# Attention and a channel mixer on one core: one more transpose by transfer, five transfers issued on ScalarE's queue, and a re-sorted order of work

## The chip, the cores and the metric

The kernel runs on one core of a Trainium2 chip. The metric is device microseconds of one execution. The names in the profile are PE (TensorE's matmuls), PEld (its weight loads), DVE (VectorE), ACT (ScalarE), POOL (GpSimd) and SP (SyncE, which here only issues transfers). An engine takes its instructions strictly in order, and an instruction that waits for a semaphore holds back all that stand behind it on its engine.

## The reference, cut to what matters

```python
# attention: q, k, v are [4, 8, 768, 64]; every query sees the first 4 keys (the sinks)
# and the last 128 keys up to its own
scores = q @ k.transpose(0, 1, 3, 2) / sqrt(64)
keep = is_sink | in_window
a = softmax(where(keep, scores, -1e9))
x = (a @ v).transpose(0, 2, 1, 3).reshape(4, 768, 512)
# mixer
h = maximum(x.transpose(0, 2, 1) @ w_tok1, 0) @ w_tok2     # over tokens, 768 -> 256 -> 768
u = x + h.transpose(0, 2, 1)
out = u + maximum(u @ w_ch1, 0) @ w_ch2                    # over channels, 512 -> 1536 -> 512
```

## The kernel before

Inputs and outputs are fp32, the matmuls work on bf16. The eight heads of each of the four batches are taken in pairs, so there are 16 pairs; pairs 0 to 3 are batch 0, pairs 4 to 7 batch 1, and so on.

Three ways bring q and k in. Pairs 0 to 3 are loaded as fp32 by transfers on SP's queue (`load_raw`, L125, tile `early`), turned into bf16 by a copy on DVE, ACT or POOL, and transposed on PE. Pairs 4 to 7 are loaded with a cast by transfers on POOL's queue and transposed on PE (L496, four 64x64 corners for each 128x128 block). Pairs 8 to 15 are loaded with a cast and transposed by a transfer on SP's queue (`turned_by_dma`, L450, tiles `qT` and `kT`). Then come the scores on PE into the PSUM tiles `ps_sc` (two of them, each read by one exponential), the exponential on ACT (L612, tile `pT`), and the product with v on PE (tile `x_sb`). The four sink rows of v for batch 0 are fetched by four small transfers into `v_sink_f` (L243); POOL casts them (L173, tile `v_sink`), and later batches copy theirs out of the tile `v_aug`, into which POOL's queue loads v.

The mixer's token step gives `u_sb` in two groups of 256 channels for batches 1 to 3 (four of 128 for batch 0). For the channel step u must stand transposed, as `uT`. Batch 0 and both groups of batch 1 are transposed on PE and copied out of PSUM by ACT or DVE (`turned_u`); both groups of batches 2 and 3 are transposed by a transfer on SP's queue (`transfer_u`, L883). The list `U_BY_DMA` names the (batch, group) that go this way. The first channel product gives `v1T`, 12 blocks by 2 halves of the tokens for each batch; its first matmul for a batch needs both groups of `uT`. The second product is plain for batch 0; for batches 1 to 3 it is done by seven quarter-size products on sums of blocks (`sums_of_v1`, `sums_of_w`). The output leaves by transfers on SP's queue (L1036 for batch 0, L1113 for the others). The last tile of batch 3 leaves in pieces as they are ready: `sc5`, 128 columns of the tile `o_sb`, is the last.

The order on all engines comes from a planner that runs while the program is built. `FIRST_BATCH` lists the PE units of batch 0's attention and token step in order. `MERGED` lists all other PE units: t0 to t73 are attention and token units, c0 to c183 channel units. `LOADS` lists POOL's loads (q, k, v and the weights T, A, C, D). For everything that isn't PE the planner picks engine and place by a cost table with assumed delays; `U_LAG` is what it assumes from the issue of a `uT` transfer to its landing. PE never departs from the listed order. Transfers of SP's and ACT's queues take eight completion semaphores in turn, so a transfer can't be issued before the one eight places earlier has landed.

Of the kernel before, what the change touches and what calls it, by code (L numbers as in the profile page):

```python
# [16 lines left out]
def kernel(  # L17
# [13 lines left out]
    nc = tc.nc  # L31
# [11 lines left out]
    D1 = D + 1  # L43
# [1 line left out]


    MERGED = (
# [11 lines left out]
    )  # L59
    FIRST_BATCH = (  # L60
        "q0 k0 m00 s00 m01 s01 q1 m02 k1 s02 m11 x1 s11 m10 q2 s10 o01 m12 k2 s12 o00 m21 q3 s21 s20 k3 o11 s22 x3 o10 "
# [1 line left out]
        "t21"  # L63
    )
    LOADS = (
        "q4 v1 v2 T0 v3 A0 C3 q5 k4 k5 C1 C0 C2 v4 q6 v5 k6 k7 q7 D2 v6 D1 D0 k8 q8 v7 q9 D3 k9 q10 k11 k10 q11 v8 v9 "
        "q12 k12 v10 v11 k13 q13 k14 q15 v12 q14 v15 v13 k15 v14"
    )
    PRODUCTS = (
        "1a 2a 1b 2b 5a 6a 5b 6b 7a 1c 7b 2c 4a 3a 4b 3b 5c 6c 7c 4c 3c"  # L70
# [6 lines left out]
    NO = 6  # L77
    BY_DMA = 8
    U_LAG = {1: 8000.0, 2: 4000.0, 3: 3500.0}
    U_BY_DMA = [(2, 0), (2, 1), (3, 0), (3, 1)]  # L80

    singles = ctx.enter_context(tc.tile_pool(name="singles", bufs=1))
    qkv_pool = ctx.enter_context(tc.tile_pool(name="qkv", bufs=NQ))
# [18 lines left out]
    in_order = tc.keep_in_program_order  # L102
# [137 lines left out]
    for n in range(4):  # L240
        i, odd = n // 2, n % 2
        rows = slice(D * i + ODD * odd, D * i + ODD * odd + n_sink)
        in_order(nc.sync.dma_start(  # L243
            out=v_sink_f[rows, odd::2, i, 0:D],
            in_=v[0].rearrange("(p o i) s d -> i o s p d", i=2, o=2)[i, odd, 0:n_sink],
        ))
        in_order(nc.vector.memset(v_sink_f[rows, odd::2, i, D:D1], 1.0))
# [564 lines left out]
    def mix_u(b, g, s0, n, by_pe=False):  # L812
        c0, cn = group(b, g)

        def run():
            ps_u = tiles["ps_u", b, g, s0] = bank("mx", n, cn)
            for st in range(n):
                if by_pe:
                    mm(ps_u[:, st], ident, x_sb[b][:, s0 + st, c0:c0 + cn], start=True, stop=False)
                for tt in range(NTOK):  # L820
                    mm(
                        ps_u[:, st], w_tok2[:, tt, ts(s0 + st, P)], tiles["mix", b][0][:, tt, c0:c0 + cn],
                        start=(tt == 0 and not by_pe), stop=(tt == NTOK - 1),
                    )

        def add(e):
            if by_pe:
                return copy(e, u_part(b, g, s0, n), tiles["ps_u", b, g, s0])
            in_order(nc.vector.tensor_tensor(  # L829
                out=u_part(b, g, s0, n), in0=tiles["ps_u", b, g, s0], in1=x_sb[b][:, s0:s0 + n, c0:c0 + cn], op=ALU.add,  # L830
            ))

        op = Op({"DVE": 150.0 + 1.05 * n * cn}, add)
        op.urgent = (1 + g) * (b == 0)
        if by_pe:
            op.cost["ACT"] = 190.0 + 0.78 * n * cn
        done["u", b, g, s0] = op
        return unit(n * (NTOK + by_pe) * cn * 0.422, run, done["h", b, g] + [done["tok2"]], {"mx": [[op]]}, [op])
# [39 lines left out]
    def transfer_u(b, g):  # L878

        for s0, n in [(0, 4), (4, 2)] if g else [(0, NT)]:  # L880
            def run(e, s0=s0, n=n):
                uT = tiles["mix", b][2].rearrange("c (g m p) -> c g m p", g=2, p=P)
                in_order(nc.sync.dma_start(  # L883
                    out=uT[:, g, 2 * s0:2 * (s0 + n)], in_=u_part(b, g, s0, n).rearrange("p t c -> p (t c)"),
                    transpose=True,
                ))

            op = Op({"SP": 230.0 * n + 400.0}, run, [done["u", b, g, u] for u in range(s0, s0 + n, 2)], lag=U_LAG[b])
            op.bulk = 440.0 * n
            for half in range(s0 // QH, (s0 + n - 1) // QH + 1):  # L890
                done.setdefault(("uT", b, half), []).append(op)
            plan.pending.append(op)
# [46 lines left out]
    def attention_and_tokens():  # L939
# [5 lines left out]
        for p in range(first, last + 1):  # L945
# [9 lines left out]
            if p == last:  # L955
                if (b, 0) in U_BY_DMA:
                    transfer_u(b, 0)
# [6 lines left out]
            if hp == 0 and p > first:  # L964
                units.append(mix_h(b - 1, 1, 0, NTOK))
                units += [mix_u(b - 1, 1, st, 2) for st in range(0, NT, 2)]
                if (b - 1, 1) in U_BY_DMA:
                    transfer_u(b - 1, 1)
                else:
                    pieces.append(turned_u(b - 1, 1))  # L970
            if hp == NHP - 1 and p < last:
                if (b, 0) in U_BY_DMA:
                    transfer_u(b, 0)
# [14 lines left out]
        units += [mix_u(b, 1, st, 2) for st in range(0, NT, 2)]  # L988
        if (b, 1) in U_BY_DMA:
            transfer_u(b, 1)  # L990
# [4 lines left out]
    def mix_channels(b):  # L995
        units, parts = [], {}
# [62 lines left out]
        def quartered(b):  # L1059
# [5 lines left out]
            units, made, steps = [], {}, {}  # L1065
# [25 lines left out]
            def columns(n, i):  # L1091
                if b == B - 1 and i == QH - 1 and n in ("3", "8"):
                    return slice(0, QC // 2) if n == "3" else slice(QC // 2, QC)
                return slice(0, QC)
# [13 lines left out]
                    op.deps.append(done[("st", *divmod(before, NT))])  # L1108
                steps[name, i] = op

            def store(st, cols, parts):
                def run(e):
                    in_order(nc.sync.dma_start(  # L1113
                        out=out[b, ds(st * P, P), cols], in_=o_buf[(b * NT + st) % NO][:, cols],
                    ))

                op = Op({"SP": 430.0}, run, parts)
                op.bulk, op.stores = 1.37 * (cols.stop - cols.start), True
                return op

            for i in range(QH):
                lo, hi = i, i + QH
                ends = b == B - 1 and i == QH - 1
                add("r1", i, lo, 0, "X", True)
                add("c1", i, lo, 0, "Z", False)
                add("r2", i, lo, 1, "X", True)
                add("c2", i, lo, 1, "Y", False, columns("3", i))
                if ends:
                    add("c5", i, lo, 1, "Y", False, columns("8", i))
                    steps["c5", i].deps.append(steps["r2", i])  # L1130
                add("r4", i, hi, 1, "X", True)
                add("c4", i, hi, 1, "Y", False)
                add("c3", i, hi, 0, "X", True)
                for later, sooner in (("c1", "r1"), ("c2", "r2"), ("c4", "r4")):
                    steps[later, i].deps.append(steps[sooner, i])
                if ends:
                    for n, st, cols in (
                        ("c1", lo, slice(0, QC)), ("c2", lo, slice(QC, QC + QC // 2)),
                        ("c5", lo, slice(QC + QC // 2, DM)), ("c3", hi, slice(0, QC)), ("c4", hi, slice(QC, DM)),
                    ):  # L1140
                        steps["s" + n, i] = store(st, cols, [steps[n, i]])
                else:
                    for st, parts in ((lo, ("c1", "c2")), (hi, ("c3", "c4"))):
                        steps["s" + parts[0], i] = done["st", b, st] = store(
                            st, slice(0, DM), [steps[n, i] for n in parts],
                        )
# [71 lines left out]
        if b in QUARTERED:  # L1218
            for j in range(0, HF, SUMMED):
                for f0 in (j, j + HF):  # L1220
                    units += [v1(ft, half) for half in range(2) for ft in range(f0, f0 + SUMMED)]
                sums_of_v1(b, j)
            return units + quartered(b)
# [91 lines left out]
    for name in LOADS.split():  # L1315
        kind, n = name[0], int(name[1:])
# [28 lines left out]
    parts = attention_and_tokens()  # L1345
# [47 lines left out]
```

## Time and profile before

| what | value |
|---|---|
| time, median of 3 runs | 195.69 us (195.45 to 195.8) |
| the profiled execution's own time | 194.44 us |
| its span, first to last instruction | 192.7 us |
| granted TensorE clock | 1.000 |
| transfers | 26.34 MB in 82138 packets |
| 128x128 PE matmuls `ps_mx<-uT,w_ch`, 384 columns | 384 of them, 69.2 us busy |

The profile is of one execution. Its page gives the busy share of each engine, then the span in 40 slices of 4.8 us each, in which each digit is the busy share in tenths. A view by windows gives the busy microseconds of each engine in chosen stretches and, in brackets, the number of instructions. The timeline lists instructions with start, length, engine, line and tiles; what stands in square brackets at the end is the idle time of the engine just before and what ended it. The chain of work that ended last runs back from the last instruction through whatever released each step. Matmuls are pipelined, so the length of one matmul in a row is longer than the distance from one to the next.

### The profile page before, as it was taken

To read this page: it belongs to the slowest core of one execution; us is meant where nothing else is said; L and a number is where in the kernel's file an instruction comes from. 1 tells how busy PE (TensorE), PEld (TensorE's weight loads), DVE (VectorE), ACT (ScalarE), POOL (GpSimd) and SP (SyncE) were. 2 spreads that over 40 slices of the span, in tenths; PEclk is the share of its full clock that TensorE was granted. 3 is DMA by queue.
4 is the path that set the end of the run, shared out by engine and by line. 5 is a ranking of instruction groups with operands and counts; after the bars stand their busy time and mean duration, and the time that the engine had idled before them with its cause. 6 is when DMAs were issued, how large, how long until landed. Compare 5 with 4: busy or idle time off the path is not lost.

```text
span 192.7 us, 5797 instructions
## 1 busy us (share of the span) xinstructions
PE 185.8 (96%) x2491; PEld 129.8 (67%) x2491; DVE 134.4 (70%) x299; ACT 106.3 (55%) x183; POOL 60.5 (31%) x78
## 2 busy tenths in 40 slices
PE   6898999999999999999999999999999999999993
PEld 1345995567764564666668888767678886567882
DVE  4768777898976647689778787847678771047672
ACT  4898767878865216879663433778642005764000
POOL 7299663765944951537810000000000000000000
PEclk9999999999999999999999999999999999999999
DMA  5999999999999999999999953400040435000016
GB/s 186 287 293 172 203 202 194 187 194 181 176 122 147 188 186 187 195 184 155 111 138 149 161 117 143 178 0 3 0 82 3 83 112 218 0 0 3 27 67 234
DMA packets 82138, 26.34 MB, mean 137 GB/s; under 512 B 69952, under 2 KB 79296, under 8 KB 82112
## 3 DMA queue, kind: packets, MB, share of 16 engines
q0 software_dynamic: 56864, 11.80, 74.8%
q1 hardware_dynamic: 25248, 14.17, 34.0%
q8 instruction: 19, 0.31, 0.7%
q14 instruction: 7, 0.06, 0.1%
HBM read 26.75 MB, written 6.29 MB: 171 GB/s over the span
## 4 chain that ended last, share of the span: by engine, by line
PE 88%; DMA 6%; DVE 1%; POOL 1%; SPq 0%; ACT 0%; issue 0%
PE ps_mx L164 77%; PE ps_sc L164 9%; DMA early<-in_q_dram 6%; PE ps_sc L496 1%; PE ps_mx L167 1%; PE ps_mx L496 1%; DVE kT L173 0%; SPq L125 0%; POOL k_bf L173 0%; POOL q_bf L173 0%; ACT qT L171 0%; POOL w_tok L182 0%; DVE o_sb L1100 0%; DVE v1T L179 0%; DVE ps_sc L545 0%
## 5 line engine op out<-in xcount | busy, mean ns | idle before, releaser
L164 PE MATMUL ps_mx<-uT,w_ch 128*128 128x384 bf16 x384 | 69.2, 326 | 0.0
L177 ACT ACTIVATE v1T<-ps_mx 128x384 bf16<-128x384 f32 x83 | 40.7, 490 | 36.1 <-PE ps_mx L164 35.5
L612 ACT ACTIVATE pT<-ps_sc 128x1024 bf16<-128x1024 f32 (+1 forms) x48 | 44.2, 954 | 19.6 <-PE ps_sc L164 19.4
L164 PEld LDWEIGHTS <-w_ch 128*128 128x128 bf16 x384 | 35.9, 98 | 21.3 <-issue 0.9
L164 PE MATMUL ps_mx<-w_ch,v1T 128*128 128x256 bf16 (+1 forms) x168 | 29.6, 318 | 0.0
L164 PEld LDWEIGHTS <-v1T 128*128 128x128 bf16 x234 | 22.5, 98 | 10.0 <-issue 0.5
L164 PEld LDWEIGHTS <-early 128*128 128x128 bf16 x222 | 21.3, 98 | 2.8
L164 PEld LDWEIGHTS <-w_tok 128*128 128x128 bf16 x240 | 19.5, 98 | 3.6 <-issue 0.2
L157 POOL DMA_DIRECT2D v_aug<-in_v_dram x16 | 16.7, 1050 | 7.5 <-PE ps_mx L164 5.1
L1255 DVE TENSOR_TENSOR early<-v1T 128x1152 bf16<-128x1152 bf16 x12 | 8.9, 754 | 13.8 <-ACT v1T L177 13.6
L829 DVE TENSOR_TENSOR u_sb<-ps_mx,x_sb 128x512 bf16<-128x512 f32 (+1 forms) x24 | 15.4, 654 | 2.9 <-PE ps_mx L164 2.6
L148 POOL DMA_DIRECT2D q_bf<-in_q_dram x16 | 13.2, 827 | 12.2 <-DMA q_bf<-in_q_dram 4.0
L164 PE MATMUL ps_mx<-w_sums,early 128*128 128x256 bf16 x126 | 15.9, 273 | 0.0
L164 PE MATMUL ps_mx<-v_aug,pT 128*128 128x65 bf16 x352 | 15.6, 193 | 0.0
L1100 DVE TENSOR_TENSOR o_sb<-ps_mx,u_sb 128x256 f32<-128x256 f32 x28 | 11.7, 422 | 5.3 <-PE ps_mx L164 5.1
L148 POOL DMA_DIRECT2D k_bf<-in_k_dram x16 | 13.3, 840 | 6.6 <-DMA v_aug<-in_v_dram 3.3
L164 PEld LDWEIGHTS <-pT 128*128 128x128 bf16 x352 | 13.8, 97 | 2.3 <-issue 0.4
L620 DVE TENSOR_TENSOR pT<-pT,mask_main 128x768 bf16<-128x768 bf16 (+1 forms) x25 | 14.6, 614 | 0.3 <-ACT pT L612 0.3
L164 PE MATMUL ps_sc<-qT,kT 64*32 64x160 bf16 (+3 forms) x480 | 14.2, 233 | 0.4 <-DVE ps_sc L545 0.2
L164 PE MATMUL ps_mx<-h1T,w_tok 128*128 128x256 bf16 (+1 forms) x120 | 14.2, 251 | 0.0
L164 PEld LDWEIGHTS <-kT 64*32 64x32 bf16 (+1 forms) x512 | 7.0, 91 | 9.1 <-issue 8.0
L164 PE MATMUL ps_mx<-x_sb,w_tok 128*128 128x256 bf16 (+1 forms) x120 | 12.2, 251 | 0.0
(84 smaller groups left out, 201.8 us busy)
## 6 DMA issues: line engine op xcount, KB each, us to landing
out_dram<-o_sb SPq DMA_DIRECT2D x22, 256.0 KB, 2.8
v_aug<-in_v_dram POOLq DMA_DIRECT2D x16, 192.0 KB, 9.4
w_ch<-in_moe_w_ch_dram POOLq DMA_DIRECT2D x8, 384.0 KB, 10.4
early<-in_q_dram SPq DMA_DIRECT2D x4, 384.0 KB, 5.2
early<-in_k_dram SPq DMA_DIRECT2D x4, 384.0 KB, 6.4
k_bf<-in_k_dram POOLq DMA_DIRECT2D x16, 96.0 KB, 11.3
q_bf<-in_q_dram POOLq DMA_DIRECT2D x16, 96.0 KB, 8.8
q_bf<-in_q_dram POOLq DMA_DIRECT2D x4, 192.0 KB, 9.4
```

What stands on the lines that cost most here:

```text
L148: in_order(nc.gpsimd.dma_start(out=out[:, h], in_=rows[:, h]))
L157: in_order(nc.gpsimd.dma_start(out=v_aug.rearrange("p i t d -> p (i t) d")[:, :, 0:D], in_=v[b].rearrange("h s d -> (h s) d")[2 * hp * S:2 ...
L164: in_order(nc.tensor.matmul(*args, skip_group_check=True, **kwargs))
L167: in_order(nc.tensor.transpose(out, in_, ident))
L177: in_order(nc.scalar.activation(out, in_, AF.Relu))
L496: in_order(nc.tensor.transpose(outs[x][columns], block, ident[rows, rows]))
L612: in_order(nc.scalar.activation(part(tiles["pT", p][:, :, ds(2 * g, 2)]), of_keys(tiles["ps_s", p, g])[:, :, 0:width(g)], AF.Exp, scale=scale,
L620: in_order(nc.vector.tensor_tensor(out=pt, in0=pt, in1=m, op=ALU.mult))
L829: in_order(nc.vector.tensor_tensor(out=u_part(b, g, s0, n), in0=tiles["ps_u", b, g, s0], in1=x_sb[b][:, s0:s0 + n, c0:c0 + cn], op=ALU.add,))
L1100: in_order(nc.vector.tensor_tensor(out=o_sb, in0=ps, in1=u_rows(b, st)[:, g, cols] if first else o_sb, op=ALU.add,))
L1255: lambda e, n=n, x=x, y=y, how=how: in_order(nc.vector.tensor_tensor(out=v1_sums[:, n, ds(j, SUMMED)], in0=of(x), in1=of(y), op=how,)), deps,
```

## The change

There are four edits.

1. `U_BY_DMA` gains (1, 0): group 0 of batch 1's u is transposed by one transfer of 12 blocks on SP's queue. The 48 matmuls of 64x64 columns on PE and the two copies out of PSUM go.
2. The four loads of the sink rows are issued by ACT instead of SP.
3. The last store, `sc5`, is issued by ACT instead of SP.
4. `MERGED` and `LOADS` are new lists of the same units and loads. `FIRST_BATCH` and `PRODUCTS` are as before.

```diff
     MERGED = (
-        "t0 t1 c20 t2 c23 c11 c22 t3 c16 c6 c0 t7 c17 c9 c1 c10 t4 c14 t5 c2 c4 t6 c5 t8 c12 t10 c21 c8 t9 t11 c13 c7 "
+        "t1 t0 c8 t2 c9 c4 c17 t3 c0 c6 c23 t7 c19 c20 c7 c2 t4 c18 c14 t5 c12 c5 t6 t8 c3 t10 c15 t9 c21 c22 t11 c1 "
...
     LOADS = (
-        "q4 v1 v2 T0 v3 A0 C3 q5 k4 k5 C1 C0 C2 v4 q6 v5 k6 k7 q7 D2 v6 D1 D0 k8 q8 v7 q9 D3 k9 q10 k11 k10 q11 v8 v9 "
+        "k4 v1 v2 T0 v3 A0 q4 C1 k5 C0 q5 C2 C3 v4 v5 q6 k7 k6 v6 q7 D0 q8 D3 k8 D1 v7 D2 q9 k9 q10 k10 q11 k11 v8 v9 "
...
-    U_BY_DMA = [(2, 0), (2, 1), (3, 0), (3, 1)]
+    U_BY_DMA = [(1, 0), (2, 0), (2, 1), (3, 0), (3, 1)]
...
-        in_order(nc.sync.dma_start(
+        in_order(nc.scalar.dma_start(
             out=v_sink_f[rows, odd::2, i, 0:D],
...
-            def store(st, cols, parts):
+            def store(st, cols, parts, by="SP"):
                 def run(e):
-                    in_order(nc.sync.dma_start(
+                    in_order((nc.scalar if by == "ACT" else nc.sync).dma_start(
                         out=out[b, ds(st * P, P), cols], in_=o_buf[(b * NT + st) % NO][:, cols],
                     ))
 
-                op = Op({"SP": 430.0}, run, parts)
+                op = Op({by: 430.0}, run, parts)
...
-                        steps["s" + n, i] = store(st, cols, [steps[n, i]])
+                        steps["s" + n, i] = store(st, cols, [steps[n, i]], "ACT" if n == "c5" else "SP")
```

The start of ACT's program before, with the semaphores waited for (DMAHW is a transfer's landing, PE and DVE are those engines):

```order
L171 ACT_TABLE_LOAD
L171 ACTIVATE q_bf<-early 128x2x6x64 [waits DMAHW0_49]
L171 ACTIVATE qT_129<-ps_mx 128x384 [waits PE_49] x2
L171 ACTIVATE kT_125<-ps_mx 128x384 [waits PE_49] x2
L612 ACTIVATE pT_133<-ps_sc_73 128x2x512 [waits PE_49]
```

The same place in the changed program:

```order
L243 DMA v_sink_f<-in_v_dram 4x2x64 [waits DVE_49]
L243 DMA v_sink_f<-in_v_dram 4x2x64 x3
L171 ACT_TABLE_LOAD
L171 ACTIVATE q_bf<-early 128x2x6x64 [waits DMAHW0_49]
L171 ACTIVATE qT_129<-ps_mx 128x384 [waits PE_49] x2
L171 ACTIVATE kT_125<-ps_mx 128x384 [waits PE_49] x2
L612 ACTIVATE pT_133<-ps_sc_73 128x2x512 [waits PE_49]
```

The four loads stand ahead of the load of ACT's function table, and the first of them waits for DVE's memset of `v_sink_f`; the table load and the first cast, `q_bf`, stand behind them.

SP's program around the new transfer of batch 1 (`qT_131` and `kT_127` are pair 10's, `qT_132` and `kT_128` pair 11's):

```order
 L450 DMA_TRANSPOSE kT_126<-k_bf 128x6x128
+L1036 DMA out_dram<-o_sb_104 128x512
+L450 DMA_TRANSPOSE qT_131<-q_bf 128x6x128
+L883 DMA_TRANSPOSE uT<-u_sb 128x12x128
+L450 DMA_TRANSPOSE kT_127<-k_bf 128x6x128
+L1036 DMA out_dram<-o_sb_102 128x512
 L1036 DMA out_dram<-o_sb_103 128x512
-L450 DMA_TRANSPOSE qT_131<-q_bf 128x6x128
+L450 DMA_TRANSPOSE qT_132<-q_bf 128x6x128
 L450 DMA_TRANSPOSE kT_128<-k_bf 128x6x128
```

The new transfer stands right behind pair 10's `qT` and ahead of pair 10's `kT`, in a row of transfers that wait for loads and for stores' data.

The end of SP's program (the pieces of the last output tiles):

```order
 L1113 DMA out_dram<-o_sb_105 128x512
-L1113 DMA out_dram<-o_sb_101 128x512
 L1113 DMA out_dram<-o_sb_103 128x128
 L1113 DMA out_dram<-o_sb_102 128x512
 L1113 DMA out_dram<-o_sb_106 128x256
-L1113 DMA out_dram<-o_sb_103 128x128
 L1388 UNCONDITIONAL_BRANCH
```

The last 128x128 store leaves SP's queue; on ACT it stands behind the last `v1T`, with nothing after it.

More of the change, by code (lines that the diff above doesn't have):

```diff
@@ L65 @@
     LOADS = (
-        "q4 v1 v2 T0 v3 A0 C3 q5 k4 k5 C1 C0 C2 v4 q6 v5 k6 k7 q7 D2 v6 D1 D0 k8 q8 v7 q9 D3 k9 q10 k11 k10 q11 v8 v9 "
-        "q12 k12 v10 v11 k13 q13 k14 q15 v12 q14 v15 v13 k15 v14"
+        "k4 v1 v2 T0 v3 A0 q4 C1 k5 C0 q5 C2 C3 v4 v5 q6 k7 k6 v6 q7 D0 q8 D3 k8 D1 v7 D2 q9 k9 q10 k10 q11 k11 v8 v9 "
+        "q12 k12 v10 v11 q13 k13 v12 v15 k15 v13 k14 q14 q15 v14"
     )
```

20 rows, old and new, of the table MERGED are left out of this document.

## The prediction

> **What bounds the kernel now.** I read the page first: the busy shares, the slices and the chain that ended last.
>
> ```profile
> span 192.7 us, 5797 instructions
> PE 185.8 (96%) x2491; PEld 129.8 (67%) x2491; DVE 134.4 (70%) x299; ACT 106.3 (55%) x183; POOL 60.5 (31%) x78
> PE   6898999999999999999999999999999999999993
> PE 88%; DMA 6%; DVE 1%; POOL 1%; SPq 0%; ACT 0%; issue 0%
> ```
>
> PE is the bound: 96% busy, nine tenths or more in nearly every slice after the fourth, and 88% of the chain. The other engines matter only where PE waits for them. A busy PE could still hide waits, so I read the view by windows, first in steps of 2 us over the start, then in long stretches. Columns: window, its length, then busy us and instruction count of PE, PEld, DVE, ACT and POOL, the clock, the DMA share and GB/s.
>
> ```profile
> 8.00:10.00 2.00, 1.69 (x27) 0.66 (x24) 1.79 (x4) 2.00 (x5) 0.90 (x2) 1.00 1.73 260
> 10.00:12.00 2.00, 2.00 (x36) 0.92 (x33) 0.54 (x2) 2.00 (x4) 2.00 (x3) 1.00 1.34 265
> 12.00:14.00 2.00, 2.00 (x42) 1.07 (x39) 1.95 (x6) 2.00 (x4) 1.85 (x3) 1.00 1.34 334
> 14.00:16.00 2.00, 1.14 (x45) 0.76 (x44) 1.16 (x3) 1.12 (x3) 2.00 (x3) 1.00 2.40 165
> 16.00:18.00 2.00, 1.78 (x42) 1.30 (x43) 1.91 (x5) 2.00 (x4) 2.00 (x4) 1.00 1.62 191
> 18.00:20.00 2.00, 2.00 (x39) 1.34 (x36) 1.97 (x6) 1.83 (x3) 2.00 (x4) 1.00 1.98 178
> 57.00:78.00 21.00, 21.00 (x323) 11.54 (x304) 13.57 (x28) 8.08 (x11) 11.43 (x13) 1.00 1.89 174
> 78.00:108.00 30.00, 30.00 (x380) 21.27 (x378) 23.80 (x48) 20.39 (x37) 11.44 (x13) 1.00 2.04 153
> 108.00:189.00 81.00, 81.00 (x855) 62.06 (x853) 52.93 (x115) 34.57 (x64) 0.00 (x0) 1.00 0.26 73
> ```
>
> Two things follow. From about 18 us to the end PE has no gap to give back: a microsecond that PE loses or saves there is a microsecond of the span. And from 8 to 14 us ACT is busy without a break; in the next 2 us it is not. So the start has a second engine at its limit, and the change puts work on exactly that engine.
>
> **The sink rows on ACT's queue.** The timeline of the start, and of 18 to 20 us:
>
> ```profile
> 0.74 1.28 ACT L171 ACT_TABLE_LOAD   x1 [0.74 <-PEq L1374]
> 2.26 0.47 SPq L125 DMA_DIRECT2D early<-in_k_dram  x1
> 2.29 0.49 DVE L239 MEMSET v_sink_f<- 128x520 f32 x1
> 2.81 1.36 SPq L243 DMA_DIRECT2D v_sink_f<-in_v_dram  x4
> 3.85 0.84 ACT L171 ACTIVATE q_bf<-early 128x768 bf16<-128x768 f32 x1 [1.83 <-DMA early<-in_q_dram]
> 4.22 0.40 SPq L125 DMA_DIRECT2D early<-in_q_dram  x1
> 9.10 0.61 POOL L173 CAST v_sink<-v_sink_f 128x520 bf16<-128x520 f32 x1 [3.51 <-DMA v_sink_f<-in_v_dram]
> 13.39 0.84 ACT L612 ACTIVATE pT<-ps_sc 128x768 bf16<-128x768 f32 x1
> 13.86 0.82 POOL L173 CAST q_bf<-early 128x768 bf16<-128x768 f32 x1
> 15.12 0.49 ACT L171 ACTIVATE qT<-ps_mx 128x384 bf16<-128x384 bf16 x1 [0.88 <-PE ps_mx L505]
> 15.51 1.94 ACT L612 ACTIVATE pT<-ps_sc 128x1024 bf16<-128x1024 f32 x2
> 17.68 0.84 ACT L612 ACTIVATE pT<-ps_sc 128x768 bf16<-128x768 f32 x1
> 18.69 0.61 PE L164 MATMUL ps_sc<-qT,kT 64*128 64x256 bf16 x8
> 19.18 1.94 ACT L612 ACTIVATE pT<-ps_sc 128x1024 bf16<-128x1024 f32 x2 [0.17 <-PE ps_sc L164]
> ```
>
> Before, ACT loads its function table at 0.74, is done at 2.02 and idles 1.83 us until the first q has landed; the table load costs nothing. In the changed order the four loads stand ahead of it and the first waits for DVE's memset, which ends at 2.78. SP issues the four from 2.81 to 4.17, 1.36 us. At that price ACT's table load runs from 4.17 to 5.45, and the first cast starts at 5.45 instead of 3.85: **ACT begins 1.60 us late**. Queued behind it are all of ACT's work of the first batch, and PE and DVE, which wait for each of its results in turn.
>
> What takes this back is ACT's own idle time. There is none until 14.23 (13.39 + 0.84), then 0.88 before 15.12 and 0.17 before 19.18: 1.05 us together. The 0.88 is a wait for PE, which waited for POOL's cast of the last q (13.86) and so for a load that does not move. So the exponential at 17.68 starts 1.60 - 0.88 = 0.72 late, and the scores that PE writes at 18.69 into the PSUM tile that this exponential reads (free at 17.68 + 0.84 = 18.52, 0.17 ahead) start 0.72 - 0.17 = **0.55 us late**. From there on PE has no gap, so this stays.
>
> Bounds: the trace has no transfer issued by ACT. If ACT issues at no more than 0.2 us each, the delay stays inside 1.05 and nothing is lost: 0. If each issue costs what SP takes for a big load, 0.47, the four take 1.9 and the loss is 1.1. I take 0.55, because the same four transfers are the nearest row. On the other side of the ledger SP is relieved of 1.36 us, but its next load (4.22) waits anyway for the first q to land, which released ACT at 3.85; at most 0.37 is won on one load, and the loads share one stream. Worth nothing in the sum. POOL's cast of the sink rows had waited 3.51 for them and may come earlier; POOL's next hard wait, the load behind 13.86, stays.
>
> **The transpose by transfer.** The chain shows the turned group as one piece, and the groups by line the copies that go with it:
>
> ```profile
> 57.23 0.53 PE ps_mx L496 x48
> L171 ACT ACTIVATE uT<-ps_mx 128x768 bf16<-128x768 bf16 x3 | 2.3, 823 | 0.0
> ```
>
> PE loses 48 matmuls and 48 weight loads, **-0.53 us** in a stretch where PE is the bound. The two copies, some 0.8 us each on ACT, lay beside PE's work (ACT is busy 8.08 of 21 us there) and bring nothing. The price is the transfer's landing. Rows of SP's queue, of the first `uT` product of batch 1 on PE, and of the median time from issue to landing:
>
> ```profile
> 53.97 1.29 DVE L829 TENSOR_TENSOR u_sb<-ps_mx,x_sb 128x512 bf16<-128x512 f32 x2 [1.05 <-PE ps_mx L164]
> 62.77 1.82 SPq L450 DMA_TRANSPOSE qT<-q_bf  x1
> 64.75 1.30 SPq L450 DMA_TRANSPOSE kT<-k_bf  x1
> 77.56 1.64 PE L164 MATMUL ps_mx<-uT,w_ch 128*128 128x384 bf16 x9
> qT<-q_bf SPq DMA_TRANSPOSE x8, 7.8
> uT<-u_sb SPq DMA_TRANSPOSE x6, 3.7
> ```
>
> u is complete at 55.3 before. The new order puts its last third behind a handful of output units, a few us later, still ahead of 62.77, where pair 10's `qT` gets its data. The `uT` transfer stands behind that one, so it is issued at about 64.65. It must have landed by 77.56: 12.9 us. Six-block transposes of that busy time land 7.8 us after issue; the quiet `uT` ones, late in the kernel, 3.7. This one has twelve blocks in the busy time, so between 7.8 and 15.6; the middle, 11.7, is in time by 1.2 us. I take 0. At the far end PE stands 15.6 - 12.9 = 2.7 us.
>
> **The last store.**
>
> ```profile
> 189.40 0.28 DVE L1100 TENSOR_TENSOR o_sb<-ps_mx,o_sb 128x128 f32<-128x128 f32 x1
> 189.51 0.33 SPq L1113 DMA_DIRECT2D out_dram<-o_sb  x1
> 189.94 0.40 SPq L1113 DMA_DIRECT2D out_dram<-o_sb  x1
> ```
>
> Its data are there at 189.68, but SP is still at the store before (189.51 + 0.33) and issues it at 189.94. An idle ACT can issue at about 189.73: **-0.2 us**; bounds are 0, where the two stores then land together, and -0.26.
>
> **The re-sorted lists.** They hold the same units with the same work, so PE's sum doesn't change; PE waits for nothing in 57 to 189 us now, so they can only add waits. I take 0. A possible place is an ACT wait such as this one, which PE did not feel:
>
> ```profile
> 106.87 0.53 ACT L171 ACTIVATE v_sink<-v_aug 4x65 bf16<-4x65 bf16 x2 [2.13 <-DMA v_aug<-in_v_dram]
> ```
>
> **The sum.** +0.55 - 0.53 - 0.2 = -0.18 us on the profiled execution, 194.44 to 194.26. The median of the runs is 195.69, 1.25 above that execution; the difference carries over, 195.5. A measurement of this kernel can tell about 0.2%, 0.39 us, from no change.
>
> **The rivals.**
>
> *Late table (slower).* The gap between 2.02 and 3.85 on ACT could hide more of the table load than its row of 1.28 shows. Once the load stands directly ahead of the first cast, whatever was hidden, up to 1.83 us, comes on top and goes straight to PE, since the 1.05 is used up: -0.18 + 1.83 = +1.65 at the far end, and with half of it, 0.92, +0.7. It decides as soon as more than 0.6 us was hidden. For it speaks only that the trace cannot exclude it; against it that no instruction stands in the gap. [...] The middle case's time is 195.69 + 0.7 = 196.4.
>
> *Late uT (slower).* The transfer shares its queue with stores and pair 10's and 11's transposes, and lands after PE gets to its first product. For it: 1.2 us of room against an uncertainty of several. Against: the listed order was made with a delay in view. Half of the 2.7: -0.18 + 1.35 = +1.2, 196.9. It decides when the transfer takes longer than 12.9 us.
>
> *Cheap issue (faster).* ACT's issues cost little, the delay at the start stays within 1.05 us, and only the gains remain: -0.53 - 0.2 = -0.73, 195.0. It decides at 0.2 us for each issue (2.81 + 0.8 + 1.28 = 4.89, which is 1.04 late). For it: only SP's price is known, and ACT may be quicker. Against: the same hardware path is asked for.
>
> *Another wait of the new order (slower).* A load or transpose that comes later by the new transfer's time holds ACT or PE: by half of the 2.13 that ACT already waits, about +0.9 in all, 196.6.
>
> **How the numbers follow.** Balance, my forecast: 0.35; its own range, with the issue from 0.3 to 0.47 us, is 195.3 to 196.1. Late table 0.15, late `uT` 0.17, other wait 0.13, cheap issue 0.2. Faster by over 0.2% is cheap issue and a twentieth from the balance: 0.25. Within 0.2% is nearly all the rest of the balance, 0.3. Slower is the remainder, 0.45: three separate mechanisms, none of which is likely alone. The range must reach the cheap issue at 195.0 with 0.1 below it, and the middles of the three slower cases, up to 196.9, with a little beyond: 194.9 to 197.1; the far ends of late `uT` and late table, about one in ten, are left out.
>
> **What would show it.** In the changed profile: the table load on ACT should start near 4.2 us and the first `q_bf` cast near 5.5 with no idle time between; PE's gap-free run should begin about half a microsecond later, with a wait for ACT at 17 to 19 us; 48 matmuls fewer on L496; no idle PE at the first `ps_mx<-uT,w_ch` of batch 1 near 77.6, with `uT` landing before it; the last store issued by ACT some 0.05 us after DVE's last addition. Idle time between the table load and the cast would speak for the late table; a cast before 5 us for the cheap issue; an idle PE anywhere after 20 us proves the zero that I took for transfer and order wrong.

## The result and the profile after

The changed kernel takes 197.95 us in the median (196.34 to 200.74, 11 executions) against 195.54 for the kernel before (11 executions beside it): a ratio of 1.0103, 95% interval 1.0079 to 1.0127. (Ratios compare undisturbed executions alone, so they are not quite the ratio of the medians.) That is slower by over 0.2%, 2.45 us above the forecast of 195.5 and above the top of its range, 197.1. The profiled execution took 197.05 us, 2.6 above the one before (194.44). The page:

```profile
span 195.3 us, 5700 instructions
PE 186.7 (96%) x2443; PEld 129.6 (66%) x2443; DVE 134.3 (69%) x301; ACT 104.1 (53%) x179; POOL 60.6 (31%) x78
PE   6698999999999999999999999999999999999993
PE 88%; DVE 5%; ACT 4%; issue 1%; ACTq 1%; DVEq 0%
```

PE is still the bound, but ACT now stands on the chain with 4% where it had 0%, and the second slice of PE reads 6 where it read 8. So the loss begins in the first 10 us. The chain of waits has one long piece that both kernels share, 77 matmuls without a wait, first before and then after:

```profile
21.57 3.85 PE ps_mx L164 x77
```
```profile
23.95 3.85 PE ps_mx L164 x77
```

By there PE is **2.38 us late**. The rest of the span adds little: 0.53 comes back where the 48 transposes are gone, 0.25 is lost near 45 us and 0.5 in the last 10 us (2.38 - 0.53 + 0.25 + 0.5 = 2.60, and the spans differ by 195.3 - 192.7 = 2.6). The start, by the timeline:

```profile
2.81 1.53 ACTq L243 DMA_DIRECT2D v_sink_f<-in_v_dram  x4
4.38 1.28 ACT L171 ACT_TABLE_LOAD   x1 [4.38 <-issue]
5.67 0.84 ACT L171 ACTIVATE q_bf<-early 128x768 bf16<-128x768 f32 x1
6.57 0.50 PE L505 MATMUL ps_mx<-ident,q_bf 64*128 64x64 bf16 x12 [1.94 <-ACT q_bf L171]
7.32 1.03 PE L164 MATMUL ps_sc<-mask_add,ident 128*128 128x512 bf16 x2
8.29 0.97 POOL L173 CAST v_sink<-v_sink_f 128x520 bf16<-128x520 f32 x1 [2.90 <-DMA v_sink_f<-in_v_dram]
9.06 1.02 ACT L612 ACTIVATE pT<-ps_sc 128x1024 bf16<-128x1024 f32 x1 [0.32 <-PE ps_sc L164]
18.20 0.22 PE L164 MATMUL ps_mx<-v_sink,pT_sink 128*128 128x130 bf16 x1 [0.45 <-DVE kT L173]
19.84 0.40 PE L164 MATMUL ps_mx<-qT,kT 64*32 64x512 bf16 x4 [0.67 <-DVE pT L620]
```

ACT does what the prediction said: issues, table load, cast, one behind the other, the cast at 5.67 where it was at 3.85. New are two things. PE stands still for 1.94 us (its "hole") between its warm-up, dummy matmuls that keep it busy before there is data, and its first transpose. And it is *slow* there: the two `mask_add` matmuls take 1.03 us. Before, the first transposes and the same two matmuls were:

```profile
4.78 0.51 PE L505 MATMUL ps_mx<-ident,q_bf 64*128 64x64 bf16 x12
5.82 0.61 PE L164 MATMUL ps_sc<-mask_add,ident 128*128 128x512 bf16 x2
```

The hole did not make PE slow in this execution. Its first transposes take 0.50 us, as before (0.51), and in executions in which PE was at full rate there they take 0.35 (s5 below). PE works slowly from the start: its warm-up weight loads begin 0.43 us apart in the changed kernel, and in s5 so up to 3.99, where from 4.38 on four take 0.75 us. So PE had not yet reached its full rate in either; before it got there by 5.82 (0.61), here only near 10 us (the transposes at 10.22 take 0.34). ACT, which was to catch up in its idle time, now waits for a slow PE (0.32 at 9.06, another 0.34 at 10.43). And PE waits for DVE at 18.20 and 19.84, where before it waited for nothing.

The transfer, by the instructions on the tile `uT`, and the first channel product of batch 1 by the timeline:

```profile
L883 SPq DMA_TRANSPOSE uT<-u_sb x1: 4982/4982/4982, 65.3 to 65.3; - x1
DMA to landing us min/median/max: 11.1/11.1/11.1
```
```profile
79.73 2.45 PE L164 MATMUL ps_mx<-uT,w_ch 128*128 128x384 bf16 x14
```

It lands at 65.3 + 11.1 = 76.4, some 3.3 us before PE asks for it, and PE does not wait. Near 45 us, the chain:

```profile
42.94 0.97 DVE kT L173
44.04 0.38 DVE ps_sc L545
44.42 0.46 DVE v1T L179
```

DVE has a long copy and a memset of PSUM to do one behind the other, where before the memset began at 41.67, well ahead; the copy out of PSUM that PE waits for (`v1T`) comes behind both. The end, by the timeline:

```profile
188.39 0.42 DVE L1100 TENSOR_TENSOR o_sb<-ps_sc,o_sb 128x256 f32<-128x256 f32 x1 [0.89 <-PE ps_sc L164]
189.50 0.50 PE L164 MATMUL ps_mx<-w_ch,early 128*128 128x128 bf16 x6
190.18 0.81 PE L164 MATMUL ps_sc<-w_ch,early 128*128 128x256 bf16 x6 [0.18 <-DVE o_sb L1100]
192.03 0.28 DVE L1100 TENSOR_TENSOR o_sb<-ps_mx,o_sb 128x128 f32<-128x128 f32 x1
192.35 0.39 ACTq L1113 DMA_DIRECT2D out_dram<-o_sb  x1
```

Here DVE first has nothing to do for 0.89 us, then too much at once, and PE waits for it. The last store leaves ACT 0.04 us after the last addition, yet the span ends 195.3 - 192.31 = 3.0 us behind that addition, as it did before (192.7 - 189.68).

### The profile page after: what moved, and what is told of

The parts are those of the page before. It is cut to its first block, busy times and chain, and to the rows that moved or that the text cites. A ratio compares the mean times of both kernels' runs of the same rounds, so it can differ in the third digit from the quotient of the medians.

```text
span 195.3 us, 5700 instructions
## 1 busy us (share of the span) xinstructions
PE 186.7 (96%) x2443; PEld 129.6 (66%) x2443; DVE 134.3 (69%) x301; ACT 104.1 (53%) x179; POOL 60.6 (31%) x78
## 4 chain that ended last, share of the span: by engine, by line
PE 88%; DVE 5%; ACT 4%; issue 1%; ACTq 1%; DVEq 0%
PE ps_mx L164 75%; PE ps_sc L164 11%; DVE kT L173 2%; ACT qT L171 1%; ACT pT L612 1%; PE ps_sc L496 1%; PE ps_mx L167 1%; PE ps_mx L505 1%; ACT L171 1%; PE ps_mx L496 1%; DVE o_sb L1100 1%; ACTq L243 1%; DVE v1T L179 0%; ACT q_bf L171 0%; ACT kT L171 0%
## 5 line engine op out<-in xcount | busy, mean ns | idle before, releaser
L164 PE MATMUL ps_mx<-uT,w_ch 128*128 128x384 bf16 x384 | 68.0, 326 | 0.1
L157 POOL DMA_DIRECT2D v_aug<-in_v_dram x16 | 16.6, 1042 | 11.8 <-DVE v1T L179 5.3
L1100 DVE TENSOR_TENSOR o_sb<-ps_mx,u_sb 128x256 f32<-128x256 f32 x28 | 11.8, 421 | 6.8 <-PE ps_mx L164 6.7
L164 PE MATMUL ps_mx<-v_aug,pT 128*128 128x65 bf16 x352 | 16.1, 193 | 0.0
```

Source lines behind the costliest of these rows:

```text
L157: in_order(nc.gpsimd.dma_start(out=v_aug.rearrange("p i t d -> p (i t) d")[:, :, 0:D], in_=v[b].rearrange("h s d -> (h s) d")[2 * hp * S:2 ...
L164: in_order(nc.tensor.matmul(*args, skip_group_check=True, **kwargs))
L1100: in_order(nc.vector.tensor_tensor(out=o_sb, in0=ps, in1=u_rows(b, st)[:, g, cols] if first else o_sb, op=ALU.add,))
```

## The experiments

Each kernel was run beside the kernel before, whose median was 195.7 to 196.1 in these comparisons; ratios are to it, with 95% intervals.

**One part at a time.** Four kernels take the change apart: the sink loads alone (before, with `nc.scalar` for `nc.sync` in the loop that loads `v_sink_f`), the changed kernel without them, the transfer alone, and the last store alone.

```diff
 s1_only_sinks    (before)   -        in_order(nc.sync.dma_start(     # v_sink_f
                             +        in_order(nc.scalar.dma_start(
 s2_sinks_back    (changed)  -        in_order(nc.scalar.dma_start(   # v_sink_f
                             +        in_order(nc.sync.dma_start(
 s3_only_ut       (before)   -    U_BY_DMA = [(2, 0), (2, 1), (3, 0), (3, 1)]
                             +    U_BY_DMA = [(1, 0), (2, 0), (2, 1), (3, 0), (3, 1)]
 s4_only_store    (before)   +    ... store(st, cols, [steps[n, i]], "ACT" if n == "c5" else "SP")
```

> The kernel before with one edit: the four sink-row loads issued by ACT. Every other engine's order is the same as before. Theory S (the start): ACT's table load falls behind the issues, the first cast starts at 5.6 to 5.7 us instead of 3.85, and the gap-free run of PE begins 2.4 us later; nothing gives it back, so +2.4 us, about 1.2% slower. Theory L (the new lists carry the loss, and part of the late start comes from the units they put there): a loss of 0.55 us as forecast, at most 1.1, so 0.3 to 0.6% slower.

> The changed kernel with the sink-row loads back on SP, all else as changed. Theory S: the start is as before; what is left is -0.5 for the transposes, +0.2 to 0.3 for a wait near 44 us and +0.5 for waits among the last products, so +0.2 us against before, the same within 0.2%. Theory L: 1.3 to 1.9 us slower than before still.

> The kernel before with one edit: group 0 of batch 1 turned by the transfer, lists as before. If the saved PE work counts in full and the transfer lands before the first product of batch 1: -0.5 us, 0.25% faster. The rival of a late transfer: PE stands at the first product of batch 1 near 77 us by up to 2.7 us, a net of 0 to +2.2 us.

> The kernel before with one edit: the last 128-column store issued by ACT. By the forecast's term -0.2 us (0.1%). By the changed kernel's trace, where ACT issued 0.04 us after the last addition but the end lay 3.0 us behind that addition as before: 0.

| kernel | median us | ratio |
|---|---|---|
| s1, sink loads alone | 197.55 | 1.0117 (1.0082 to 1.0153) |
| s2, all but the sink loads | 195.98 | 1.0025 (0.9992 to 1.0059) |
| s3, transfer alone | 196.29 | 1.0037 (1.0010 to 1.0064) |
| s4, last store alone | 195.85 | 1.0012 (0.9983 to 1.0042) |

The loss is the sink loads. Moving one small group of transfers costs 1.2%; everything else together costs too little to tell from nothing. The last store shows no gain, though its interval leaves room for the 0.2 us of the forecast. The transfer alone is slower by 0.4%, where a gain of 0.25% was forecast. In its trace the time of the 48 matmuls is won (0.51), and PE does not wait for `uT`, and yet DVE and PE wait later for loads on POOL's queue:

```profile
80.86 0.38 DVE L173 COPY v_sink<-v_aug 4x65 bf16<-4x65 bf16 x2 [2.43 <-DMA v_aug<-in_v_dram]
86.03 0.30 PE L164 MATMUL ps_mx<-v_sink,pT_sink 64*128 64x65 bf16 x8 [1.42 <-DVE x_sb L722]
```

Whether the transfer's traffic made these loads late is not shown: this execution, at 197.78, was the slowest of twelve.

**Why the start costs three times the forecast.** Two theories. *Late ACT*: everything queues behind ACT's late cast. *Clock*: PE loses its granted clock in the hole of about 2 us. The trace of s1, by windows (the column behind POOL is the clock):

```profile
6.00:8.00 2.00, 1.06 (x26) 0.52 (x26) 0.58 (x3) 1.56 (x4) 0.00 (x0) 0.93 1.07 335
8.00:10.00 2.00, 1.72 (x10) 0.42 (x12) 1.12 (x2) 1.63 (x3) 0.67 (x2) 0.50 1.68 239
10.00:12.00 2.00, 2.00 (x34) 1.06 (x30) 0.62 (x2) 1.44 (x3) 2.00 (x3) 0.50 1.34 280
12.00:14.00 2.00, 1.64 (x13) 0.37 (x10) 2.00 (x3) 1.38 (x3) 1.79 (x2) 0.50 1.43 319
14.00:16.00 2.00, 2.00 (x38) 1.04 (x35) 0.73 (x2) 2.00 (x4) 1.57 (x3) 0.87 2.30 172
```

Here, other than in the changed kernel's trace, PE had the full clock (0.60 for the two `mask_add` matmuls at 7.04), lost it just behind the hole, and had half of it until after 14 us. The next two kernels are s1 with one part of the mechanism taken away: s5 fills the hole with more warm-up matmuls and leaves ACT late; s6 lets ACT load its table first and so starts the cast at 4.40.

```diff
 s5_sinks_warm (s1)   -    keep_warm(7, 0)
                      +    keep_warm(12, 0)
 s6_sinks_table (s1)  +    table = singles.tile([P, 1], BF16)
                      +    in_order(nc.scalar.activation(table, ones[:, 0:1], AF.Copy))
```

> Before with the four sink loads on ACT, and 12 warm-up matmuls instead of 7, so that PE does not stand still while the cast is late. Theory late ACT: the loss of the sink edit (2.3 us in the run with that edit alone) is ACT's late cast and what queues behind it; PE's idle time meant nothing, and the time stays near 198.0, perhaps 0.2 more for the longer warm-up. Theory clock: about half of the loss, 1.0 to 1.3 us, is PE at half speed from 7.7 to 14.5 us because it had stood still for 2 us; with the hole filled PE is at full speed by about 9 us, and the time is 196.6 to 197.0.

> Before with the four sink loads on ACT, and one ACT copy of a single column of ones ahead of them, so that the function table is loaded before the loads are issued. Both theories of the start agree that the first cast then comes at about 4.35 instead of 5.67 (0.5 late against before), which is inside ACT's idle 1.05 us. Late ACT: at most 0.3 us over before, 195.7 to 196.1. Clock: PE still stands still 0.5 us longer than before, which can cost the full clock in more of the executions: 196.0 to 196.6. If it stays at 198 the issues cost something else than the place of the table load.

s5 takes 195.87 us, ratio 1.0006 (0.9978 to 1.0035): no loss is left to see, though ACT's cast is as late as in s1 (5.69). s6 takes 196.31, ratio 1.0010 (0.9971 to 1.0049). In s5 PE is at full speed at once behind a hole of half the length (lines between these are left out):

```profile
6.58 0.35 PE L505 MATMUL ps_mx<-ident,q_bf 64*128 64x64 bf16 x12 [0.96 <-ACT q_bf L171]
7.04 0.60 PE L164 MATMUL ps_sc<-mask_add,ident 128*128 128x512 bf16 x2
19.53 0.61 PE L164 MATMUL ps_sc<-qT,kT 64*128 64x256 bf16 x8
```

Neither theory gave a number as low as 195.87 for s5; the clock theory had the sign right and half of the size.

**The hole without a late ACT.** s10 is the kernel before with a shorter warm-up; nothing but PE is touched.

```diff
 s10_cold (before)    -    keep_warm(7, 0)
                      +    keep_warm(3, 0)
```

> Before with 3 warm-up matmuls instead of 7 and nothing else: no engine but PE is touched, ACT's first cast stays at 3.85, and PE stands still for about 1.9 us ahead of its first real matmul. Theory clock: the hole alone costs what the sink edit cost; PE is at half speed until 10 us or later, and the time is 196.8 to 197.8. Theory late ACT: with ACT in time nothing is lost, 195.5 to 196.0.

195.81 us, ratio 0.9996 (0.9967 to 1.0025). The clock theory said 196.8 to 197.8 and **is wrong as it stood**: a hole of 1.93 us costs nothing while ACT is in time.

**Both together, without any transfer on ACT's queue.** If neither a late ACT nor a hole costs anything alone, either the two cost it together, or the transfers on ACT's queue do something of their own. s14 makes ACT late by six needless copies; s15 is the same with the hole filled; s16 is the whole change with the table loaded first, as in s6.

```diff
 s14_act_busy (before)        +    for _ in range(6):
                              +        in_order(nc.scalar.activation(o_buf[NO - 1], ones, AF.Copy))
 s15_act_busy_warm (s14)      -    keep_warm(7, 0)
                              +    keep_warm(12, 0)
```

> Before with six needless ACT copies of ones (into an output tile that is overwritten later) ahead of the first cast; the sink loads stay on SP. ACT is then free for the first cast at about 5.7 to 5.9 instead of 3.85, as late as with the sink loads on its queue. Theory both (a late ACT and PE's hole of 2 us together cost the clock): 197.3 to 198.2. Theory queue (the transfers on ACT's queue do something more than delay): 195.9 to 196.6, the price of the late ACT alone.

> The same with 12 warm-up matmuls, so that PE has next to no hole. Theory both: the loss goes, 195.8 to 196.3. Theory queue: no difference between this kernel and the one without the longer warm-up.

> The changed kernel with one ACT copy of a single column ahead of its four sink loads, so that the function table is loaded first; the first cast comes at 4.4 instead of 5.67, PE's hole is 0.7 instead of 1.94 us. Theory both: as with the sink edit alone, where this took 1.2 us away, 196.3 to 196.8, and what is left over before is half ACT's 0.5 and the new order's waits of 0.7 less the transposes' 0.5. If the table's place is not the cause: 197.8 to 198.1.

With before, s10 and s13 (below) this is a table of two causes, each there or not. The last column counts executions whose mean granted clock was under 0.995.

| kernel | ACT's first cast | PE's hole | median us | ratio | low clock |
|---|---|---|---|---|---|
| s13 | in time (3.92) | 0.15 | 195.68 | 0.9991 (0.9968 to 1.0014) | 1 of 12 |
| s10 | in time (3.96) | 1.93 | 195.81 | 0.9996 (0.9967 to 1.0025) | 0 of 12 |
| s15 | late (5.89) | 0.66 | 196.00 | 1.0016 (0.9986 to 1.0046) | 0 of 12 |
| s14 | late (5.89) | 2.14 | 197.64 | 1.0102 (1.0068 to 1.0136) | 6 of 10 |

So it is the two together, whatever makes ACT late. s14 has no transfer on ACT's queue and costs what the change costs. But the number of warm-up matmuls sets two things, the hole and how long PE has been busy ahead of it. No run with an ACT as late changes one without the other, so "hole" in this table stands for both.

The low clock goes with the loss: 6 of 11 executions of the changed kernel, 4 of 6 of s1, 7 of 12 of s7 (below), and none of 36 of the three kernels with ACT as late and the hole filled (s5, s11, s15). The kernel before has it in 10 of the 125 executions beside these. Where it lies is known for the profiled executions alone: behind the hole in s1 and s14, in the changed kernel's nowhere in its first 190 us, and in s7's only from 20.8 to 24.2 us, where PE had waited for DVE for 0.45 and 1.05 us:

```profile
20.00:22.00 2.00, 1.57 (x16) 0.86 (x17) 1.26 (x4) 0.84 (x2) 1.22 (x2) 0.69 1.30 201
22.00:24.00 2.00, 1.72 (x21) 1.18 (x22) 0.32 (x1) 1.01 (x2) 0.82 (x2) 0.50 1.30 202
24.00:26.00 2.00, 2.00 (x37) 1.66 (x35) 1.44 (x5) 1.28 (x3) 1.02 (x1) 0.96 1.32 203
```

Two places in the timeline show how the two add up: the first small product on the sinks, and the scores that before were written at 18.69. Before (the first place), s10 (hole), s15 (late ACT) and s14 (both), in this order, with the lines between left out:

```profile
9.81 0.40 PE L164 MATMUL ps_mx<-qT,kT 64*32 64x512 bf16 x4
```
```profile
6.27 1.04 PE L164 MATMUL ps_sc<-mask_add,ident 128*128 128x512 bf16 x2
11.43 0.41 PE L164 MATMUL ps_mx<-qT,kT 64*32 64x512 bf16 x4
19.46 0.61 PE L164 MATMUL ps_sc<-qT,kT 64*128 64x256 bf16 x8
```
```profile
11.41 0.40 PE L164 MATMUL ps_mx<-qT,kT 64*32 64x512 bf16 x4
19.71 0.61 PE L164 MATMUL ps_sc<-qT,kT 64*128 64x256 bf16 x8
```
```profile
7.22 0.61 PE L164 MATMUL ps_sc<-mask_add,ident 128*128 128x512 bf16 x2
9.00 1.03 PE L164 MATMUL ps_sc<-mask_add,ident 128*128 128x512 bf16 x2
12.62 0.41 PE L164 MATMUL ps_mx<-qT,kT 64*32 64x512 bf16 x4
20.92 0.61 PE L164 MATMUL ps_sc<-qT,kT 64*128 64x256 bf16 x8
```

Against the execution before, s10 is 1.62 late and then 0.77; s15 1.60 and then 1.02; s14 2.81 and then 2.23. Each delay alone finds 0.6 to 0.85 us of idle time to hide in. Together they find 0.58 in all: the slack is there once. But s10's delay is not its hole's own: s4, in which nothing at the start was touched, shows the same `mask_add` row and is 1.55 and then 1.22 late (11.36 and 19.91). What s10 stands for here is a PE that reaches its full rate late.

s2 and the changed kernel, which differ in the sink loads alone, say the same. In both profiled executions PE is slow at first (1.03 for the `mask_add` matmuls); the first cast comes at 4.00 and 5.67, and the 77 matmuls begin at 22.20 and 23.95. Of ACT's 1.67 us nothing is absorbed. In s11, the changed kernel with 12 warm-up matmuls and PE at full rate (below), they begin at 22.96. So what decides is whether PE is at full rate while ACT should catch up. With 7 warm-up matmuls and a late ACT it had not reached it (the changed kernel, s7) or lost it again (s1, s14); with 12 it had it in all three traces (s5, s11, s15).

s16 takes 196.68, ratio 1.0036 (1.0004 to 1.0068): 1.3 us of the change's loss go with the place of the table load alone.

**The changed kernel with the hole filled, and the lists of before.**

```diff
 s11_after_warm (changed)  -    keep_warm(7, 0)
                           +    keep_warm(12, 0)
 s7_lists_back (changed)   MERGED and LOADS of before
```

> The changed kernel with 12 warm-up matmuls instead of 7. Theory clock: what it lost over before goes as it went with the sink edit alone (197.55 to 195.87, so -1.7); the transposes' -0.5 and the new order's waits of 0.7 stay: 196.0 to 196.4, and 0.3 above the kernel with the sink edit and 12 warm-ups at most. Theory late ACT: 197.6 to 198.2, as the changed kernel.

> The changed kernel with the lists MERGED and LOADS of before. Theory lists help the transfer: without the new order the uT transfer pushes back POOL's loads of v, as it did in before with the transfer alone; the time is that of the sink edit plus the transfer, 197.6 + 0.6 = 198.2 to 198.8, above the changed kernel's 197.95. Theory lists hurt: the new order only added waits (0.25 at 45 us, 0.5 at the tail); then this is 197.2 to 197.5, below the changed kernel.

s11: 196.34 us, ratio 1.0034 (1.0009 to 1.0059), so five more warm-up matmuls take 1.6 us from the median of the changed kernel (0.7%, some 1.35 us, by the ratios). s7: 197.66, ratio 1.0076 (1.0043 to 1.0108), between what the two theories gave, and its interval overlaps the changed kernel's: whether the new lists help or hurt is **not settled**. The waits for v that s3's trace shows are not in s7's profiled execution, so they do not come every time with the transfer and these lists.

**A better version.** s9 puts the last 22 channel units of s2 back into the order that before has; s12 adds two warm-up matmuls to it, and s13 adds the same two to before.

```diff
 s9_tail (s2)              c162 to c183 of MERGED in before's order
 s12_best (s9)             -    keep_warm(7, 0)
                           +    keep_warm(9, 0)
 s13_before_warm (before)  the same
```

> The changed kernel with the sink loads back on SP, and the last 22 channel units (c162 to c183) in the order that before has. Theory tail: the 0.5 us that PE and DVE lose from 185 us on comes from c173 standing late among these units; it goes, and the time is 195.98 - 0.45 = 195.5 (195.3 to 195.7), with no PE wait for DVE's o_sb in the last 8 us. Theory elsewhere: the tail's loss belongs to something earlier (a late transfer or copy), and the time stays at 195.9 to 196.1.

> The sink loads back on SP, the last 22 channel units in before's order, the transfer for u and the last store as changed, and 9 warm-up matmuls instead of 7. Theory clock: two more matmuls fill the 0.2 to 0.5 us holes ahead of the first transposes, the full clock comes by 8 us in more executions, and up to 1.2 us goes against 0.3 us of later start: 194.8 to 195.3, with fewer executions above 196. If the clock's moment does not depend on holes this small: 195.9 to 196.1.

> Before with 9 warm-up matmuls instead of 7 and nothing else. Theory clock: 195.0 to 195.5 with fewer executions above 196, 0.2 to 0.3 above the kernel with the same warm-up that also saves the 48 transposes. If holes this small do not matter: 195.9 to 196.2, by the later start.

s9: 195.75, ratio 0.9984 (0.9955 to 1.0014); the time lies between the two forecasts and does not decide. In its tail the two products that stood 0.68 us apart in the changed kernel (189.50 and 190.18) follow each other in 0.33 with no wait:

```profile
188.56 0.50 PE L154 MATMUL ps_mx<-w_ch,early 128*128 128x128 bf16 x6
188.89 0.82 PE L154 MATMUL ps_sc<-w_ch,early 128*128 128x256 bf16 x6
```

s12: 195.38, ratio 0.9981 (0.9957 to 1.0006); s13: 195.68, ratio 0.9991 (0.9968 to 1.0014). Both medians lie between what the two theories gave. s12 beats the changed kernel clearly (1.0103 against 0.9981); that it beats the kernel before is likely but not shown.

## Why the prediction was wrong

**The start, +0.55: this is the step that failed.** Its parts were right one by one. The four issues took 1.53 us on ACT (1.36 taken from SP), the cast came 1.82 late (1.60), and with PE at full clock its subtraction comes out in s5 and s15, which have before's lists. In s5 ACT is 1.84 late (5.69) and the scores of 18.69 come 0.84 late (19.53), where 1.84 - 1.05 = 0.79; in s15 it is 2.04 (5.89) and 1.02, where 2.04 - 1.05 = 0.99. What failed is that the 1.05 us of idle time can be taken off at all in most executions. Two things were not in it. PE's hole was not looked at: the prediction followed ACT's lateness along ACT and asked of PE only when it would get its data, not at what speed it would then work. And ACT's idle time was read from one execution in which PE had the full clock early. In the profiled executions of s2, s3, s4 and s9, whose sink loads and warm-up are before's, the two `mask_add` matmuls take 1.03 or 1.04 us, as in s10, and not 0.61.

So in four of the five profiled executions with this start a slow PE already uses that idle time, and a late ACT comes on top of it. With the low clock that more than half of the executions have, this makes 0.55 into 1.8 by medians (s1, 197.55 against 195.74 beside it) and 2.3 by the ratio (1.17% of 195.74). The three slower rivals, 0.45 together, did not have this mechanism.

The carry-over of 1.25 us from the profiled execution to the median was a right number and an unasked question: its size is that of the late clock (at the scores of 18.69 the four kernels named are 0.6 to 1.4 late, s10 0.77), so it may well have pointed at the thing that mattered. That it is the clock alone is not shown. In s12's profiled execution PE had its full rate early, but the first k landed late (DVE's cast at 6.80, before at 4.89), and the 77 matmuls begin at 23.80, 2.23 behind before's. And s13, whose two more warm-up matmuls should win back what a late clock costs, is not shown to be faster: 0.6 us at most, by its interval.

**The transposes, -0.53:** right; the shift of PE drops by 0.53 there in the changed kernel.

**The landing of `uT`, 0:** right. Issued at 65.3 (64.65 was forecast), landed after 11.1 us (11.7). That the middle of so wide a range, 7.8 to 15.6, came this close is partly luck. The 3.3 us to spare are mostly PE's own lateness: in s2, whose start is in time, the transfer lands at 66.0 + 10.9 = 76.9 and PE asks at 77.91, 1.0 us later (1.2 was forecast). Loads of v wait up to 2.43 us in s3, which has the transfer; in the changed kernel's profiled execution they do not.

**The last store, -0.2:** not seen. It is issued 0.04 us after the addition, as forecast, but the span ends 3.0 us behind the addition as before: from the issue to the end it is 2.95 us (195.3 - 192.35), where it was 2.76 (192.7 - 189.94). Why is open. s4 alone: 1.0012 (0.9983 to 1.0042).

**The lists, 0:** wrong by 0.75 in the traces. The 0.25 near 45 us and the 0.5 in the tail are the rival of another wait, whose 0.9 was about right in size, with other places: not a load or a transpose but DVE, to which the new order gives its work in bursts. s9's trace shows the tail's part; the other stays a reading of the trace.

**The other rivals.** Late table: false; the cast starts at 5.67 where the table load ends (4.38 + 1.28 = 5.66). Cheap issue: false; 1.53 / 4 = 0.38 us an issue, above the 0.2 from which it decides. Late `uT`: false, with 3.3 us to spare, and 1.0 in s2.

Three things stay open. The hole and the short warm-up are not told apart: five more matmuls change both. How often the clock comes late in executions that were not profiled can't be read from their mean clock: in the changed kernel's trace every window of 2 us up to 190 us reads 1.00, also where the `mask_add` matmuls take 1.03. And executions of the changed kernel with a mean clock of 0.995 or more are slow too (five of them, 197.86 in the median), so the low means are a sign of the cause and not all of its cost.

## What to carry to other kernels

When an edit makes the first work of a kernel late, ask what the idle matmul engine does meanwhile: here a matmul engine that was slow behind a short warm-up and a hole of 2 us made a delay that is worth 0.8 to 1.0 us cost about twice that, and five more dummy matmuls, or a one-column activation that pulls the function table load ahead of the transfers, took nearly all of it back. Idle time that a profile shows can be spent once, and one profiled execution may show it unspent: compare its own time with the median first, and if they differ by more than the effect that is forecast, find out by what. To test a cause that needs two conditions, run all four combinations; each of the two alone looked innocent.

## What the runs showed of the hardware

The granted clock after a warm-up. In s14 PE had the full clock at 7.22 (0.61 for the two `mask_add` matmuls) in spite of a hole of 2.14 us just before, and half of it at 9.00 (1.03); the windows have the clock itself:

```profile
6.00:8.00 2.00, 1.06 (x26) 0.52 (x26) 0.31 (x2) 1.56 (x4) 0.00 (x0) 1.00 0.94 295
8.00:10.00 2.00, 1.54 (x8) 0.30 (x10) 1.11 (x2) 1.68 (x4) 0.84 (x2) 0.58 1.58 279
10.00:12.00 2.00, 2.00 (x35) 1.09 (x34) 0.74 (x2) 1.52 (x3) 2.00 (x3) 0.56 1.48 254
```

So in s14 the clock fell after the hole, not in it. At a clock of 0.5 (s1's windows from 8 to 14 us read 0.50) the means give (0.42 + 0.44) x 2 / 0.5 = 3.4 us of half rate in s14 (8.3 to 11.8); s1, by its rows above, had (0.07 + 3 x 0.5 + 0.13) x 2 / 0.5 = 6.8 us (7.7 to 14.5), and s7 (0.31 + 0.50 + 0.04) x 2 / 0.5 = 3.4. These lengths are estimates from the means; what sets them is not shown. Nor is what sets the moment of the full rate: with one and the same start the two `mask_add` matmuls took 0.61 us at 5.82 in before and 1.04 at 6.27 in s4. Holes of 2.06 (s1) and 2.14 us (s14), behind warm-ups of 3.07 and 3.17 us, were followed by the half rate. In both the clock fell, by these estimates, in a second, short wait of PE (0.63 us, until 8.28 and 8.46), so it need not have been the hole alone.

ACT's table load stands directly ahead of its first activation, behind transfers that ACT issued earlier: in the changed kernel at 4.38, behind the four issues from 2.81 to 4.34 and ahead of the cast at 5.67. In s6, where an activation of one column stands ahead of the four, the table load is at 0.74 and their issue begins at 2.81. And another queue is not shown to bring the sink rows sooner: POOL's cast of them came at 8.29 in the changed kernel and at 9.33 in s1, and with the loads on SP's queue at 9.10 before, 8.66 in s3 and 10.22 in s4.
